# A planned attention kernel: another overlap for ScalarE in the planner, paddings moved in the opening, a new settings string

## The chip, the cores and the metric

The kernel runs on one core of a Trainium2 chip. The metric is the device time of one execution in microseconds; less is better. The time of the kernel before is the median of three runs.

## What is computed

The input is x, 2048 tokens of 512 numbers, in bfloat16. Two blocks are applied in turn, and the pair of them twice:

```python
x = x + A(layernorm(x), wqkv, wo)
x = x + B(layernorm(x), w1, b1, w2, b2)
x = x + A(layernorm(x), wqkv, wo)
x = x + B(layernorm(x), w1, b1, w2, b2)
```

A is softmax attention over all tokens with 32 heads of 16 numbers each: queries, keys and values come from one product with wqkv, the scores are scaled by 16 to the power -0.5, the probabilities weigh the values, and wo maps the result back. B is a product with w1 (512 by 1376), bias, tanh-approximated gelu, a product with w2, bias. The weights are the same in both rounds.

## The kernel before, in words

**Tiles.** Four heads make a head group; there are eight. Queries come in units of 512 tokens (smaller at the very end), keys in blocks of 128. One score tile is 128 keys by 512 queries of one head of a group. TensorE makes it with a 32-row product (line 1586) into a PSUM bank. There are 4096 such tiles in all.

**Two ways to the exponential.** Most tiles go to ScalarE: `flow_scores` takes them in groups, alternately of three banks and of two, and one ACTIVATE (line 1571) turns a group into probabilities in `PT`. Tiles whose key block is in `DK` (five of sixteen) can go to VectorE instead: `take_d` (line 1600) picks one, line 1678 writes its bits, and lines 1664, 1665, 1710, 1711 and 1719 add three shifted copies, which are used with scaled values `vs`. TensorE then multiplies probabilities with values (line 1805) and sums in bank `ACCB`. VectorE also does statistics, scaling and copies; GpSimd makes some shifts and the powers behind the layer norms.

**The order of the work.** Everything is planned when the kernel is built. `Sched` simulates five engine queues with durations written into the code, picks the earliest ready task with the lowest priority number, and writes the instructions of each engine in that order; on the chip every engine works its list in this order and waits on semaphores. A `Task` is submitted with its priority; `n0` (that is `now0`) puts an instruction into the list at once. `Prog.op` (line 109) computes when an engine is free again: the start plus the duration less `OVERLAP` of the engine (line 161). An exponential of n banks has the duration 0.19 + 0.4275 n. `best`, `stay` and `scores_due` use the same number to judge when ScalarE will want its next scores.

**The settings string.** `Hint.ORDER` has one digit for every four exponential groups (`STEP`, line 1504). A digit names an entry of `MODES`, which changes a few limits: how idle VectorE must be to be given a tile, when values are multiplied, how long other work may hold scores up. Digit 9 lets a group of three give one of its banks to a VectorE tile. A step beyond the string uses entry 0.

**Fills.** `refill` puts products of zeros (`zw`) into gaps of TensorE, into `ACCB` or a spare bank. Its `put` counts them at double duration while the plan's time is below `COLD`.

**The opening.** `build_startup` (line 808) issues the loads on SP in the order x tiles 0, 1, 2-3, weights of the keys, of the queries, of the values, x 4 to 9. GpSimd writes constants. The buffers `qk` 0 to 5 hold a tile's queries and keys, 16 numbers per head in 32 places, so the holes of 16 must be zero and one column of ones must stand in each key's hole: that is `pads` (line 845). GpSimd pads buffers 0 and 1, and ScalarE 2 to 5 with a copy of zeros (VectorE sets the ones); between them GpSimd sets the column of ones in V (line 862). Then come the statistics of x (line 983, 984), their scale on GpSimd (lines 991, 992), the scaling on VectorE (line 1003), transposes on TensorE (line 1161), their copy by ScalarE (line 1162), the products for keys, queries and values (line 1181), the keys' transposes by SP's DMA queue (line 1185), the bounds and scales of `job_scl`, the first scores and the first exponential. `job_first_tile` does this for tiles 0 to 3; each takes a `qk` buffer from the pool of line 736.

Of the kernel before, what the change touches and what calls it, by code (L numbers as in the profile page):

```python
# [13 lines left out]
ACTF = mybir.ActivationFunctionType  # L14
# [4 lines left out]
NDMAQ = 24  # L19
LATENCY = {"act": 0.033, "dve": 0.034, "pool": 0.083, "pe": 0.053, "sp": 0.06}  # L20
LAT_PE = 0.174
OVERLAP = {"act": 0.1415, "dve": 0.083, "pool": 0.014}
PE_SWITCH = 0.107
PE_ISSUE = 0.0035
DMA_MARGIN = 0.8
# [40 lines left out]
class Prog:  # L66
# [42 lines left out]
    def op(self, eng, fn, reads=(), writes=(), same_ok=(), dur=0.3, lat=None):  # L109
# [33 lines left out]
        else:  # L143
# [16 lines left out]
            op.t1 = op.t0 + dur  # L160
            self.free[eng] = op.t0 + (max(0.02, dur - OVERLAP[eng]) if lat is None else lat)
        deps = {}
# [121 lines left out]
def I(fn, reads=(), writes=(), dur=0.3, same_ok=(), lat=None):  # L284
    return (fn, tuple(reads), tuple(writes), tuple(same_ok), dur, lat)
# [9 lines left out]
class Sched:  # L295
# [147 lines left out]
    def stay(self, f, lim):  # L443

        P = self.P
        act = P.free["act"] + sum(max(0.02, o[4] - OVERLAP["act"]) for t in self.pend["act"] for o in t.ops)
        dve = P.free["dve"] + sum(o[4] for t in self.pend["dve"] if self.task_ready(t) <= f + D_NEAR for o in t.ops)
# [14 lines left out]
    def scores_due(self, f, lim):  # L462
# [7 lines left out]
        if first is None or first - f > HOLD_REACH:  # L470
            return None
        act = self.P.free["act"] + sum(max(0.02, o[4] - OVERLAP["act"]) for t in self.pend["act"] for o in t.ops)
        return max(first, act - HOLD_LEAD) + HINT.HOLD_LATE
# [67 lines left out]
FILL_LEAST = 96  # L541
FILL_MOST = 448
FILL_W = 3.414
COLD = 6.0
FILL_DT = 0.05
FILL_U = 0.55
FILL_SLACK = 0.02
# [12 lines left out]
ACCB = 6  # L560
# [28 lines left out]
class Hint:  # L589
    BASE = dict(D_IDLE=1.2, PV_LEAST=0.75, HOLD_LATE=0.4, PV_NEAR=0.7, LIN2=9, D_STEAL=0, POST=0, POOL_SHIFT=1, PV_DEEP=2, DEFER=0.0)  # L590
    MODES = (dict(), dict(D_IDLE=0.8), dict(D_IDLE=1.7), dict(PV_LEAST=0.6), dict(PV_LEAST=0.9), dict(HOLD_LATE=0.2), dict(HOLD_LATE=0.6), dict(PV_NEAR=0.4), dict(LIN2=0.9), dict(D_STEAL=1.0), dict(POST=1), dict(POST=2), dict(POOL_SHIFT=0), dict(DEFER=-2.0), dict(DEFER=0.2), dict(PV_DEEP=4, PV_LEAST=0.85), dict(PV_DEEP=3, PV_LEAST=0.8), dict(PV_DEEP=4, PV_LEAST=0.85, HOLD_LATE=0.7))
    STEP = 4
    ORDER = '5774500h8h000900700000440501000f04010f407c9f1c0hc700000b43cb00c4009084070hc200204040ccgg43c08f0900000c8c0cc0020c900342h003050234300373ffeda000h0004d2f00g30c3700700f0hgd0c9f5907e04h0770000h0203000000c003327h730000cf09277010g3047204c03f000de84c3025090fh9800c00000e9ec90f309020004803000c0000c9400c40g0cfh030009gf0003'

    def mode(self, k):
        self.__dict__.update(self.BASE)
# [2 lines left out]
    def at(self, step):  # L599
        self.mode(int(self.ORDER[step], 36) if step < len(self.ORDER) else 0)  # L600

# [5 lines left out]
class Builder:  # L607
# [45 lines left out]
    def alloc(self, es):  # L653
# [75 lines left out]
        pl = self.S_.pools  # L729
# [3 lines left out]
        pl["dp"] = Pool((0, 2, 4, 6) + tuple(range(12, NDP, 2)))  # L733
        pl["qraw"] = Pool(range(2))
        pl["qt"] = Pool(range(3))
        pl["qk"] = Pool(range(6))
        pl["vst"] = Pool([])
        pl["xn"] = Pool(range(3))
        pl["xnT"] = Pool(range(3))
# [68 lines left out]
    def build_startup(self):  # L808
        S, NT, NFC = self.S, self.NT, self.NFC
        n0 = self.now0  # L810
# [22 lines left out]
                self.S_.mark(("xld", a))  # L833
        self.S_.spawn(late(), 1.7)

        pool = lambda fn, writes, dur=0.4, reads=(): n0("pool", I(fn, reads, writes, dur))
        dve = lambda fn, reads, writes, dur=0.14: Task("dve", 1.9, [I(fn, reads, writes, dur)])
        pool(lambda e: e.memset(self.cneg[:, :], -0.5), [("cneg",)])
        pool(lambda e: e.memset(self.cstep.bitcast(U16)[:, :], SHIFT[1]), [("cstep",)])
# [5 lines left out]
        def pads(eng, b):  # L845
            qv = self.qks(b)
            hole = qv.rearrange("p k (h c) -> p (k h) c", c=32)[:, :, 16:32]
            ones = I(lambda e: e.memset(qv[:, 1, :].rearrange("p (h c) -> p h c", c=32)[:, :, 16:17], 1.0), [], [("qk", b, 0), ("qk", b, 1)], 0.1)
            if eng == "act":
                n0("act", I(lambda e: e.activation(out=hole, in_=self.zw[:, 0:16].unsqueeze(1).broadcast_to([128, 64, 16]), func=ACTF.Copy), [("zw",)], [("qk", b, 0), ("qk", b, 1)], 1.05))  # L850
                self.S_.submit(Task("dve", 1.3, [ones]))
            else:
                n0("pool", I(lambda e: e.memset(hole, 0.0), [], [("qk", b, 0), ("qk", b, 1)], 0.6),
                   I(ones[0], ones[1], ones[2], 0.2))
        n0("dve", I(lambda e: e.memset(self.zw[:, :], 0.0), [], [("zw",)], 0.2))
        n0("dve", I(lambda e: e.tensor_scalar(out=self.ident[:, :], in0=self.ioi, scalar1=0.0, scalar2=None, op0=ALU.is_equal), [("ioi",)], [("ident",)], 0.3))
        n0("dve", I(lambda e: e.memset(self.ps[:, ACCB, :], 0.0), [], [("ps", ACCB)], 0.57))  # L857
        self.P.free["act"] = 2.0
        vv = self.V[:, :, :, :, :].rearrange("p g k h d -> p (g k h) d")
        for b in (0, 1):  # L860
            pads("pool", b)
        n0("pool", I(lambda e: e.memset(vv[:, :, 16:17], 1.0), [], [("V", hg, kb) for hg in range(8) for kb in range(16)], 0.6))
        for b in range(2, 6):
            pads("act", b)

        def consts():
# [502 lines left out]
    def refill(self):  # L1369
# [5 lines left out]
        def add(act, t0, t1, w):  # L1375
            k = int(t0 / FILL_DT)
            while t0 < t1 - 1e-9:
                e = min(t1, (k + 1) * FILL_DT)
                act[k] += (e - t0) * w
                t0, k = e, k + 1  # L1380
# [23 lines left out]
        def put(b, how, p, w, st):  # L1404
            z = self.zero(b, how, p, w, st)
            x = P.op("pe", z[0], z[1], z[2], z[3], z[4] * (2.0 if P.free["pe"] < COLD else 1.0), z[5])
            add(real, x.t0, x.t1, 1.0 if how == "full" else 0.25)

        def fill(op):
# [8 lines left out]
            for t0, b, st, due in banks(op, start, t - op.t0)[:1]:  # L1418
                e = min(end, due)
                while True:  # L1420
                    rate = 1200.0 if t0 < COLD else 2400.0
                    w = min(FILL_MOST, int((e - t0) * rate))
# [814 lines left out]
```

## Time and profile before

| | |
|---|---|
| runs | 1533.81 us median of 3 (1532.12 to 1535.83) |
| profiled execution | 1530.92 us, of which the span of its instructions is 1529.1 us |
| TensorE busy | 1478.3 us (97%), fills among it |
| VectorE busy | 1388.9 us (91%) |
| ScalarE busy | 1493.3 us (98%) |
| GpSimd busy | 626.0 us (41%) |
| exponential groups on ScalarE | 1250, 1415.3 us |
| tiles on VectorE | 998 |

Busy time counts an instruction from start to end with overlaps counted once. In the groups, the number behind the bar is the busy time and the mean of one instruction in nanoseconds; behind the second bar stands the idle time just ahead of these instructions and what ended it. PE is TensorE, PEld its weight loads, DVE VectorE, ACT ScalarE, POOL GpSimd, SP the queue that issues the DMAs. PEclk is the clock granted to TensorE as a share of the full one.

### The profile page before, as it was taken

The page shows a single profiled execution, that of the slowest core. Times are in us where ns is not written, and L with a number is a line of the kernel's source. Part 1 is how long each engine was busy: PE and PEld are TensorE (multiplying, and loading weights), DVE is VectorE, ACT ScalarE, POOL GpSimd, SP SyncE. Part 2 cuts the span into 40 slices and gives each one's busy share as a digit, 9 for nine tenths or more (in the row PEclk, how much of TensorE's full clock was granted, in tenths as well). Part 3 has the DMA queues.
Part 4 walks back from the last instruction along what each step waited for, and adds up shares of the span by engine and source line. Part 5 has one row for each costly group of instructions (what it writes and reads, how often), then busy time and mean ns, then how long its engine had stood idle before and what let it go on. Part 6 is the DMA issues. An engine that isn't in the chain of part 4 may idle for free.

```text
span 1529.1 us, 49040 instructions
## 1 busy us (share of the span) xinstructions
PE 1478.3 (97%) x21518; PEld 516.5 (34%) x21518; DVE 1388.9 (91%) x2516; ACT 1493.3 (98%) x1339; POOL 626.0 (41%) x854
## 2 busy tenths in 40 slices
PE   8999999999999999999999999999999999999998
PEld 3322333333223322332233332223222332444664
DVE  7889999989999899989999798999999978998895
ACT  7999999999999999999999999999999999999996
POOL 4675653234343143434454437543444312441220
PEclk9999999999999999999999999999999999999999
DMA  5762111223221222213742332210011001120331
GB/s 154 123 143 76 57 32 36 57 32 87 78 50 46 48 79 60 57 36 90 135 81 63 61 89 56 63 35 13 22 36 36 20 24 31 40 44 19 81 64 27
DMA packets 212517, 91.05 MB, mean 60 GB/s; under 512 B 182251, under 2 KB 207184, under 8 KB 212304
## 3 DMA queue, kind: packets, MB, share of 16 engines
q1 hardware_dynamic: 212304, 87.92, 25.2%
q8 instruction: 168, 2.75, 0.8%
q14 instruction: 45, 0.37, 0.1%
HBM read 36.81 MB, written 19.48 MB: 37 GB/s over the span
## 4 chain that ended last, share of the span: by engine, by line
ACT 46%; PE 38%; DVE 13%; issue 2%; POOL 1%; DVEq 0%; POOLq 0%
ACT PT L1571 44%; PE ps L1586 12%; PE ps L1805 12%; PE ps L1892 11%; DVE dp L1678 5%; DVE dp L1719 2%; ACT h L2004 1%; PE ps L1479 1%; DVE dp L1665 1%; DVE st L983 1%; DVE accT L1835 1%; PE ps L1475 1%; DVE h L1981 0%; DVE dp L1710 0%; PE ps L1797 0%
## 5 line engine op out<-in xcount | busy, mean ns | idle before, releaser
L1571 ACT ACTIVATE PT<-ps 128x1536 bf16<-128x1536 f32 (+1 forms) x1250 | 1415.3, 1290 | 16.9 <-PE ps L1586 15.2
L1678 DVE TENSOR_SCALAR dp<-ps 128x512 uint16<-128x512 f32 x998 | 661.3, 681 | 76.6 <-PE ps L1586 68.7
L1586 PE MATMUL ps<-QT,KT 32*128 32x512 bf16 (+2 forms) x5120 | 597.4, 339 | 22.2 <-ACT PT L1571 8.6
L1711 POOL TENSOR_TENSOR dp<-dp,cstep 128x512 int32<-128x512 int32 x278 | 289.0, 1039 | 642.6 <-DVE dp L1678 417.2
L1805 PE MATMUL ps<-PT,V 128*17 128x512 bf16 (+2 forms) x3873 | 499.1, 339 | 2.7 <-issue 2.3
L1805 PE MATMUL ps<-dp,vs 128*17 128x512 bf16 (+2 forms) x3741 | 477.9, 338 | 1.2 <-issue 0.6
L1586 PEld LDWEIGHTS ps<-QT,KT 32*128 32x128 bf16 x5120 | 170.1, 91 | 516.4 <-ACT PT L1571 267.2
L1719 DVE TENSOR_SCALAR dp<-dp 128x2048 uint16<-128x2048 uint16 (+1 forms) x387 | 265.2, 694 | 5.8 <-POOL dp L1711 2.1
L1805 PE MATMUL ps<-dp,V 128*17 128x512 bf16 (+2 forms) x1247 | 233.2, 338 | 1.5 <-DVE accT L1835 0.9
L1805 PEld LDWEIGHTS ps<-dp,vs 128*17 128x17 bf16 x3741 | 133.2, 89 | 126.2 <-issue 90.4
L1805 PEld LDWEIGHTS ps<-PT,V 128*17 128x17 bf16 x3873 | 134.1, 89 | 97.8 <-issue 75.7
L1479 PE MATMUL ps<-zw 128*32 128x448 bf16 (+21 forms) x1627 | 166.8, 323 | 0.0
L1477 PE MATMUL ps<-zw 32*128 32x448 bf16 (+6 forms) x410 | 126.8, 333 | 0.0
L1892 PE MATMUL ps<-yT,wf 128*32 128x512 bf16 (+2 forms) x1720 | 109.3, 339 | 4.6 <-issue 2.4
L1892 PE MATMUL ps<-wqkv,xnT 128*32 128x512 bf16 x1392 | 101.4, 381 | 2.8 <-DVE dp L1678 0.8
L1311 POOL TENSOR_SCALAR QT<-qraw,scl,qbias 128x512 bf16<-128x512 bf16 (+2 forms) x91 | 76.7, 843 | 54.1 <-PE ps L1586 52.5
L1475 PE MATMUL ps<-zw 128*128 128x448 bf16 (+15 forms) x313 | 77.6, 333 | 4.7 <-DVE ps L857 3.0
L1665 DVE TENSOR_SCALAR dp<-dp 128x4096 uint16<-128x4096 uint16 x60 | 74.2, 1237 | 0.1
L1805 PEld LDWEIGHTS ps<-dp,V 128*17 128x17 bf16 x1247 | 60.3, 89 | 37.2 <-issue 18.5
L1479 PEld LDWEIGHTS ps<-zw 128*32 128x32 bf16 x1627 | 58.5, 95 | 21.4 <-issue 2.7
L1981 DVE TENSOR_SCALAR h<-ps,b1c 128x512 bf16<-128x512 f32 (+4 forms) x88 | 57.5, 654 | 8.5 <-PE ps L1892 7.8
L1835 DVE STREAM_TRANSPOSE accT<-ps 128x512 f32<-128x512 f32 (+2 forms) x96 | 59.4, 619 | 5.8 <-PE ps L1805 5.3
(202 smaller groups left out, 1119.6 us busy)
## 6 DMA issues: line engine op xcount, KB each, us to landing
vs<-vs_scr SPq DMA_DIRECT2D x64, 255.0 KB, 2.8
wf<-in_B_w_dram SPq DMA_DIRECT2D x90, 128.0 KB, 2.6
q_scr<-qk SPq DMA_DIRECT2D x20, 256.0 KB, 2.1
k_scr<-qk SPq DMA_DIRECT2D x12, 256.0 KB, 2.0
out_dram<-xres SPq DMA_DIRECT2D x16, 128.0 KB, 1.7
vs_scr<-vs SPq DMA_DIRECT2D x8, 255.0 KB, 3.1
xres<-in_A_x_dram SPq DMA_DIRECT2D x7, 256.0 KB, 5.5
v_scr<-vst SPq DMA_DIRECT2D x12, 136.0 KB, 2.3
```

Of the source, the lines that this page charges most:

```text
L1311: yield Task(eng, 0.4, [I(lambda e: e.tensor_scalar(out=self.QT[:, q, 0:W], in0=src, scalar1=self.scl[:, k, hg:hg + 1], scalar2=self.qbias ...
L1475: fn = lambda e: e.matmul(self.ps[:, b, 0:w], lhsT=self.zw[:, 0:128], rhs=self.zw[:, 0:w], start=st, stop=st, skip_group_check=True)
L1477: fn = lambda e: e.matmul(self.ps[:, b, 0:w], lhsT=self.zw[32 * p:32 * p + 32, 0:128], rhs=self.zw[32 * p:32 * p + 32, 0:w], start=st, sto ...
L1479: fn = lambda e: e.matmul(self.ps[32 * p:32 * p + 32, b, 0:w], lhsT=self.zw[:, 0:32], rhs=self.zw[:, 0:w], start=st, stop=st, skip_group_c ...
L1571: S_.submit(Task("act", 1e-5 * gi, [I(lambda e, pt=pt, n=n, b0=b0: e.activation(out=self.PT[:, pt:pt + n, :], in_=self.ps[:, b0:b0 + n, :] ...
L1586: return [I(lambda e, kb=kb, i=i: e.matmul(self.ps[:, b, i * W:(i + 1) * W], lhsT=self.KT[32 * hp:32 * hp + 32, hg, kb * 128:(kb + 1) * 12 ...
L1665: return lambda e: e.tensor_scalar(out=self.both(x[1], y[1]), in0=self.both(x[0], y[0]), scalar1=float(SHIFT[2]), scalar2=None, op0=ALU.add)
L1678: self.S_.submit(Task("dve", 0.0, [I(lambda e: e.tensor_scalar(out=self.dpu(u)[:, w * 512:(w + 1) * 512], in0=self.ps[:, b, :], scalar1=BI ...
L1711: lambda e: e.tensor_tensor(out=self.dpu(u + 1).bitcast(I32), in0=self.dpu(u).bitcast(I32), in1=self.cstep[:, 0:1].broadcast_to([128, 512] ...
L1719: t = Task("dve", prio(), [I(lambda e: e.tensor_scalar(out=self.dpp(v)[:, :, 0:N], in0=self.dpp(u)[:, :, 0:N], scalar1=float(SHIFT[2]), sc ...
L1805: ops.append((nth[j, sh] + 0.1 * i, I(lambda e, hp=hp, v=v, ap=ap[:, i * W:(i + 1) * W], first=first and i == 0, W=W: e.matmul(self.ps[32 ...
L1892: return [I(lambda e, j=j: e.matmul(self.ps[32 * j:32 * j + 32, b, 0:W], lhsT=lhsT(slice(32 * j, 32 * j + 32)), rhs=rhs(), start=start, st ...
```

## The change

The planner's overlap for ScalarE goes from 0.1415 to 0.128 us and `COLD` from 6.0 to 6.4. The settings string is another one, 312 digits instead of 313. In the opening, VectorE clears bank `ACCB` ahead of making the identity; V's ones are written by ScalarE, as a copy of a one-element constant, and not by GpSimd; buffers 0, 1, 4, 5 are padded by VectorE, buffer 0 at once and the others as tasks with priority 2.2 and more; ScalarE pads 2 and 3. The pool of `qk` buffers begins with 0, 2, 3, and 1, 4, 5 join it once they are padded. The planned duration of GpSimd's constants is 0.1 instead of 0.4.

```diff
-OVERLAP = {"act": 0.1415, "dve": 0.083, "pool": 0.014}
+OVERLAP = {"act": 0.128, "dve": 0.083, "pool": 0.014}
...
-COLD = 6.0
+COLD = 6.4
...
-    ORDER = '5774500h8h000900700000440501000f04010f407c9f1c0hc7...
+    ORDER = '57054000dh0003f3ff04f03207330700c002077c23c00ff4h0...
...
-        pl["qk"] = Pool(range(6))
+        pl["qk"] = Pool((0, 2, 3))
...
-        pool = lambda fn, writes, dur=0.4, reads=(): n0("pool", I(fn, reads, writes, dur))
+        pool = lambda fn, writes, dur=0.1, reads=(): n0("pool", I(fn, reads, writes, dur))
...
             else:
-                n0("pool", I(lambda e: e.memset(hole, 0.0), [], [("qk", b, 0), ("qk", b, 1)], 0.6),
-                   I(ones[0], ones[1], ones[2], 0.2))
+                zero = I(lambda e: e.memset(hole, 0.0), [], [("qk", b, 0), ("qk", b, 1)], 0.5)
+                if b == 0:
+                    n0("dve", zero, ones)
+                else:
+                    self.S_.submit(Task("dve", 2.2 + 0.01 * b, [zero, ones]), cb=lambda: self.S_.release("qk", b))
         n0("dve", I(lambda e: e.memset(self.zw[:, :], 0.0), [], [("zw",)], 0.2))
+        n0("dve", I(lambda e: e.memset(self.ps[:, ACCB, :], 0.0), [], [("ps", ACCB)], 0.48))
         n0("dve", I(lambda e: e.tensor_scalar(out=self.ident[:, :], in0=self.ioi, scalar1=0.0, scalar2=None, op0=ALU.is_equal), [("ioi",)], [("ident",)], 0.3))
-        n0("dve", I(lambda e: e.memset(self.ps[:, ACCB, :], 0.0), [], [("ps", ACCB)], 0.57))
         self.P.free["act"] = 2.0
         vv = self.V[:, :, :, :, :].rearrange("p g k h d -> p (g k h) d")
-        for b in (0, 1):
-            pads("pool", b)
-        n0("pool", I(lambda e: e.memset(vv[:, :, 16:17], 1.0), [], [("V", hg, kb) for hg in range(8) for kb in range(16)], 0.6))
-        for b in range(2, 6):
+        n0("dve", I(lambda e: e.memset(self.onec[:, :], 1.0), [], [("onec",)], 0.1))
+        n0("act", I(lambda e: e.activation(out=vv[:, :, 16:17], in_=self.onec[:, :].unsqueeze(1).broadcast_to([128, 512, 1]), func=ACTF.Copy), [("onec",)], [("V", hg, kb) for hg in range(8) for kb in range(16)], 2.38))
+        for b in (0, 1, 4, 5):
+            pads("dve", b)
+        for b in (2, 3):
             pads("act", b)
```

## Rows read from the trace of the kernel before

**Rows 1.** Profile page: the chain that ended last, shares of the span by line.

```profile
ACT PT L1571 44%; PE ps L1586 12%; PE ps L1805 12%; PE ps L1892 11%; DVE dp L1678 5%; DVE dp L1719 2%; ACT h L2004 1%; PE ps L1479 1%; DVE dp L1665 1%; DVE st L983 1%; DVE accT L1835 1%; PE ps L1475 1%; DVE h L1981 0%; DVE dp L1710 0%; PE ps L1797 0%
```

**Rows 2.** By stretches: each engine's busy us (instructions), then PEclk, DMA share, GB/s.

```profile
0.00:22.90 22.90, 16.71 (x95) 8.40 (x95) 17.38 (x53) 14.59 (x26) 8.29 (x22) 1.00 0.65 183
...
100.00:1450.00 1350.00, 1318.69 (x18040) 439.46 (x18036) 1250.28 (x2206) 1338.77 (x1184) 552.30 (x721) 1.00 0.23 54
...
6.60:8.40 1.80, 0.00 (x0) 0.00 (x0) 1.80 (x8) 0.00 (x0) 1.04 (x3) 1.00 1.09 365
```

**Rows 3.** Profile page, costliest groups: ScalarE's exponentials, VectorE's loads and shifts.

```profile
L1571 ACT ACTIVATE PT<-ps 128x1536 bf16<-128x1536 f32 (+1 forms) x1250 | 1415.3, 1290 | 16.9 <-PE ps L1586 15.2
L1678 DVE TENSOR_SCALAR dp<-ps 128x512 uint16<-128x512 f32 x998 | 661.3, 681 | 76.6 <-PE ps L1586 68.7
...
L1719 DVE TENSOR_SCALAR dp<-dp 128x2048 uint16<-128x2048 uint16 (+1 forms) x387 | 265.2, 694 | 5.8 <-POOL dp L1711 2.1
```

**Rows 4.** Timeline of ScalarE, 450 to 520 us: start, us, line, operation, count.

```profile
450.49 42.80 ACT L1571 ACTIVATE PT<-ps 128x1536 bf16<-128x1536 f32 x38 [0.28 <-PE ps L1586]
```

**Rows 5.** Groups by shape on ScalarE in that run of exponentials.

```profile
L1571 ACT ACTIVATE PT<-ps 128x1536 bf16<-128x1536 f32 x18 | 27.1, 1506 | 0.3 <-PE ps L1586 0.3
L1571 ACT ACTIVATE PT<-ps 128x1024 bf16<-128x1024 f32 x20 | 21.4, 1090 | 0.0
```

**Rows 6.** Waits: who for whom, total us, times, longest.

```profile
PEld ps L1586 <- DVE dp L1678: 63.4, 182, 0.9
...
ACT PT L1571 <- PE ps L1586: 15.2, 33, 1.9
```

**Rows 7.** Timeline of the opening: start, us, engine, line, operation, count, idle before.

```profile
0.84 0.24 DVE L855 MEMSET zw<- 128x224 uint32 x1 [0.84 <-PEq L2222]
...
1.21 1.17 DVE L856 TENSOR_SCALAR ident<-dp 128x128 bf16<-128x128 f32 x1
...
2.01 2.00 ACT L850 ACTIVATE h<-zw 128x1024 bf16<-128x1024 bf16 x2
2.11 1.57 SPq L818 DMA_DIRECT2D wqkv<-in_A_wqkv_dram  x3
...
3.03 3.54 PE L1475 MATMUL ps<-zw 128*128 128x448 bf16 x9 [3.03 <-DVE ps L857]
3.14 0.66 DVE L983 BATCH_NORM_STATS2 st<-xres 128x6 f32<-128x512 bf16 x1 [0.17 <-issue]
...
3.56 2.37 POOL L862 MEMSET V<- 128x512 bf16 x1
...
4.30 0.32 DVE L984 BATCH_NORM_AGGREGATE mv<-st 128x2 f32<-128x6 f32 x2
...
4.66 0.48 DVE L867 MEMSET dp<- 128x512 uint32 x1
...
6.02 0.19 POOL L991 TENSOR_SCALAR rs<-mv 128x1 f32<-128x1 f32 x1
...
6.29 0.60 POOL L992 TENSOR_TENSOR rs<-rs,cneg 128x1 f32<-128x1 f32 x1
...
8.00 0.38 DVE L1003 TENSOR_SCALAR dp<-xres,mv,rs 128x512 bf16<-128x512 bf16 x1
...
9.09 1.09 ACT L1162 ACTIVATE yT<-ps 128x512 bf16<-128x512 bf16 x2 [3.19 <-PE ps L1161]
...
9.83 1.87 PE L1181 MATMUL ps<-wqkv,yT 128*128 128x512 bf16 x4 [0.35 <-ACT yT L1162]
...
21.28 1.04 PE L1181 MATMUL ps<-wqkv,yT 128*128 128x512 bf16 x4
...
22.85 8.26 ACT L1571 ACTIVATE PT<-ps 128x1536 bf16<-128x1536 f32 x7
```

**Rows 8.** DMA issues of the opening: count, KB each, median us to landing.

```profile
wqkv<-in_A_wqkv_dram SPq DMA_DIRECT2D x3, 512.0 KB, 6.3
...
xres<-in_A_x_dram SPq DMA_DIRECT2D x2, 128.0 KB, 2.1
```

More of the change, by code (lines that the diff above doesn't have):

```diff
@@ L592 @@
     STEP = 4
-    ORDER = '5774500h8h000900700000440501000f04010f407c9f1c0hc700000b43cb00c4009084070hc200204040ccgg43c08f0900000c8c0cc0020c900342h003050234300373ffeda000h0004d2f00g30c3700700f0hgd0c9f5907e04h0770000h0203000000c003327h730000cf09277010g3047204c03f000de84c3025090fh9800c00000e9ec90f309020004803000c0000c9400c40g0cfh030009gf0003'
+    ORDER = '57054000dh0003f3ff04f03207330700c002077c23c00ff4h01004bb9cb9c1cc009803000e9g17h09700f0f04gb0804c00330c4fc8cg340cd00057h332ff0fc00aef000cca4053037d00f30200c007c01c4170gc0df72c40023c44g0030f0092d00000cdc0c700c00983c9h010c02019433c021cc9303g090g307h009f44b72ch00gb40c04d00c13ch3450513cdcc1900491c0b48090000d49470000'
     def mode(self, k):
```

## The prediction

> **What bounds the kernel now.** I read four views, from coarse to fine. The chain of waits [rows 1] runs through ScalarE's exponentials (line 1571) for 44% of the span; the matmul lines hold much of the rest because a group's scores stand just ahead of its exponential. The view by stretches [rows 2] says it more sharply: from 100 to 1450 us ScalarE works 1338.77 of 1350 us, so only 11.2 us are left idle there, while VectorE works 1250.28 and has 99.7 us free. In the first 22.9 us nothing is exponentiated at all; ScalarE works 14.59 of them. So the time is an opening of 22.9 us, then ScalarE's list of instructions back to back, then a tail that the diff doesn't touch. A gain can come from an earlier first exponential, from a shorter list (tiles handed to VectorE), or from ScalarE's 15.2 us of waiting for scores [rows 6].
>
> **Part 1, the opening.** In the timeline of the opening [rows 7] the reader should follow one chain: x's statistics are done (4.30 + 0.32 = 4.6), but GpSimd takes up the scale of tile 0 only at 6.02, because it is still writing V's ones (3.56 + 2.37 = 5.93). The scaling on VectorE starts at 8.00, ScalarE's copy of the transposed tile at 9.09, the first key product at 9.83, the first exponential at 22.85.
>
> Removed from GpSimd: two paddings with their ones, and V's ones. With them gone only short constants stand ahead of the scale, which then waits for the statistics alone. Two things replace it.
>
> VectorE takes paddings 0, 1, 4, 5. Padding 0 stands ahead of the statistics: start 0.84, zeros 0.24, the accumulator's zeros 0.5, the identity, one constant 0.1, the padding 0.5 (for it and the accumulator the 128x512 memset of 0.48 is the nearest row), its ones 0.1. The identity took 1.17 in a stretch where GpSimd wrote a padding; I take 0.38, which is what the scaling at 8.00 cost, with 1.17 as the other end. That ends at 2.7, or at 3.5. The statistics of x's tile 0 started at 3.14 with VectorE idle for 0.17 ahead of them, so x came just then: at 0.38 this wait covers the padding; at 1.17 the statistics slip by 0.4. Paddings 1, 4, 5 come with priority 2.2, behind statistics and constants: 3 x 0.6 = 1.8 us in a stretch where VectorE has 22.9 - 17.4 = 5.5 us free [rows 2]. If that cover fails, they cost up to 1.8; behind them stands the fourth tile, whose buffer 1 isn't free before.
>
> ScalarE loses paddings 4 and 5 (two take 2.00) and gains V's ones. No row shows that write on ScalarE: the ends are 0.6 (a 128x512 tile on it, as at 9.09: two in 1.09) and 2.37 (GpSimd, the same scattered write). I take the upper, since it is the same pattern. Then ScalarE is free at 2.0 + 2.4 + 2.0 = 6.4, otherwise at 4.6.
>
> New chain: scale at 4.6 instead of 6.02, its two GpSimd instructions 0.9 as before (6.02 to 6.9), scaling at 5.5, plus 1.09 to ScalarE's copy = 6.6 (ScalarE is free at 6.4), plus 0.74 to the key product = 7.3. What is late next: the key weights. Their issue starts at 2.11; the three weights have one landing figure, 6.3 [rows 8]. As the third one's (three issues in 1.57, so its own starts near 3.2) it means 9.5, and two loads of 0.52 MB at 365 GB/s [rows 2] take 2.9, so the first lands at 6.6. Ends: 4.2 (the 2.1 of x's tiles) and 9.5. At 6.6 it doesn't bind. So the key product comes at 7.3 instead of 9.83: 2.5 us. Bounds: 0.4 if the weights bind at 9.5, 3.2 if all is in time at 6.6.
>
> **The clock.** The first four key products take 1.87, four alike at 21.28 take 1.04, all in stretches where the granted-clock column reads 1.00. The spacing tells more than the column: nine fills of 448 columns take 3.54, that is 0.39 each, the 1.2 GHz level; TensorE then stands from 6.57 to 8.45. The accumulator's zeros now come ahead of the identity, so fills can start at 1.6 instead of 3.03 and last until the transposes. If that brings the key products to 2.4 GHz, it adds 1.87 - 1.04 = 0.8. The fills here didn't bring it over the pause, so I leave it out of the sum and keep it as the upper end, and as a rival. The Trainium skill (TensorE: Matmul & The Clock Gate, What's actually happening) says that the default is the slow clock and that activity releases it; by that rule the opening gives 3.3 instead of 2.5.
>
> From the first key product to the first exponential are 13.0 us, which I leave as they are: statistics of keys, queries, the DMA transposes on SP and the scale all shift along; the number of SP's instructions is unchanged. Opening: -2.5, between -4.0 (3.2 + 0.8) and +1.4 (0.4 gained, 1.8 lost to the paddings).
>
> **Part 2, the account and the string.** OVERLAP is what the planner takes off an exponential's duration for the start of the next. 18 three-bank and 20 two-bank groups [rows 5] ran in 42.80 [rows 4]. By the code a group is 0.19 + 0.4275 per bank, together 47.41; with 37 overlaps the old constant gives 42.17, the new 42.67. The new one fits. Over 1250 groups the planner had ScalarE 1250 x 0.0135 = 16.9 us too early. With the same instructions the constant changes nothing on the chip; it works through the order that the planner writes.
>
> What the order can win: an exponential costs 1415.3 / 1250 = 1.13 us a group [rows 3], with 2.5 tiles in a group on average 0.45 per tile. A tile on VectorE costs it (661.3 + 265.2) / 998 = 0.93 us, from the same groups. If the planner sees ScalarE 16.9 us longer, balance returns at 16.9 / (0.45 + 0.93) = 12 tiles moved, worth 5.5 us, against 99.7 us free. Second reading: the string has one digit for four groups; 313 digits for 1250 groups before, 312 after, so at most 1248 and at least 1245 groups: 2 to 5 fewer, 2.3 to 5.7 us, provided tiles per group stay (the digit that shrinks groups, 9, stands 15 times before, 16 times after). I take the middle of this, -4.0; the ends are 0 (the length says nothing) and -5.7, and -7.6 more if half of the 15.2 us of waiting goes.
>
> From the same rows the overlap is (47.41 - 42.80) / 37 = 0.125. The Trainium skill (ScalarE: Activation LUTs, What ACT_TABLE_LOAD costs) says that back-to-back activations overlap by about 93 ns; by that the new constant would leave the planner 0.035 x 1250 = 44 us short, still misjudging ScalarE. The trace disagrees with it, at 125.
>
> COLD, the GpSimd duration and the smaller qk pool are the planner's alone; they cost nothing beside what is counted.
>
> **Sum.** -2.5 - 4.0 = -6.5 on the profiled execution's 1530.92 gives 1524.4. The median of the runs shown is 2.9 above that execution, so I put the forecast at 1533.8 - 6.5 = 1527.3. About 0.2% (3.1 us) is what a measurement of this kernel can tell from no change.
>
> **Rivals.** (a) *Opening alone*: the new order wins and loses alike, and only -2.5 stays: 1531.3, no change to be told. For it: ScalarE has 11.2 us idle in 1350, little to win without moving tiles. Against: the digits. Chance 0.15. (b) *An account still short*: waits hide in the 42.80 us the other way, the real spacing is wider than the new constant, the order stays as ill-fitting as it was, and again 1531.3. Against it: 42.67 and 42.80 are 0.3% apart. Chance 0.05. The Trainium skill's 93 ns, cited above, would be this case. (c) *Late weights*: the key weights land at 9.5, the opening gives 0.4, the order 4.0: 1529.4. Chance 0.10. (d) *Fast clock from the start*: the longer fills bring the key products to 2.4 GHz, 0.8 more: 1526.5. For it: fills could start 1.4 us earlier; against it: they ran 3.54 us before and the products were still slow. Chance 0.12. The Trainium skill's clock gate, cited above, speaks for it. (e) *More tiles moved*: 20 tiles rather than 9 go into VectorE's free 99.7 us: -2.5 - 20 x 0.45 = -11.5, 1522.3. Chance 0.10. (f) *Slower*: more VectorE tiles put more of their scores ahead of ScalarE's groups in TensorE's fixed order. TensorE already waits 182 times on VectorE's loads, and ScalarE 33 times for scores, 15.2 / 33 = 0.46 us each [rows 6]. If these double, +15.2 - 6.5 = +8.7: 1542.5. It decides from 14 more such waits (14 x 0.46 = 6.4), and is told from no change from 21. Against it: an account that fits makes late arrivals rarer. Chance 0.13. The forecast keeps 0.35.
>
> Faster: 0.35 + 0.10 + 0.12 + 0.10 = 0.67; same 0.15 + 0.05 = 0.20; slower 0.13. The range goes from 1533.8 - 4.0 - 5.7 - 7.6 = 1516.5, put at 1517, to 1533.8 + 1.4, put at 1535; it leaves out (f) and little else.
>
> **What would show it.** Right: GpSimd's first scale near 4.6, ScalarE free near 6.4, first key product near 7.3, first exponential near 20.3; 1245 to 1248 groups and some 1003 to 1010 VectorE tiles; ScalarE's waits for scores at or below 15.2. V's ones far above 2.4 would show the opening step wrong; a first exponential at 22 with the key product at 7.3 would show that the chain behind it sets the opening. More than 1250 groups, or waits for scores above 22, would make the prediction wrong.

## The result and the profile after

The kernel after takes 1536.61 us (median of 20 executions, 1533.98 to 1539.54); the kernel before took 1533.98 us beside it (20 executions, 1531.98 to 1536.79). The ratio is 1.0016, interval 1.0009 to 1.0023: slower by about 2.5 us, inside the 0.2% that I called indistinguishable, and outside the range given, on the side where the prediction had left rival (f) out. The profiled execution of after took 1538.27 us (span 1536.2), 1.7 above its median, while that of before lies 3.1 below its own. So the two traces differ by more than the two kernels do, and what follows rests on pairs of rows and on medians, not on the two spans.

Four lines of the page of after answer to [rows 1, 3]: the chain by line, then the groups (busy us, mean ns | idle before them, and who ended it).

```profile
ACT PT L1575 21%; PE ps L1590 15%; PE ps L1809 14%; PE ps L1896 13%; DVE dp L1682 11%; DVE dp L1723 3%; DVE dp L1669 2%; PE ps L1479 2%; PE ps L1483 1%; ACT h L2008 1%; DVE st L987 1%; DVE accT L1839 1%; DVE dp L1714 1%; PE ps L1185 1%; DMA yT<-xn 1%
...
L1575 ACT ACTIVATE PT<-ps 128x1536 bf16<-128x1536 f32 (+1 forms) x1247 | 1414.9, 1266 | 26.6 <-PE ps L1590 22.8
L1682 DVE TENSOR_SCALAR dp<-ps 128x512 uint16<-128x512 f32 x1009 | 669.3, 681 | 73.4 <-PE ps L1590 65.2
...
L1723 DVE TENSOR_SCALAR dp<-dp 128x2048 uint16<-128x2048 uint16 (+1 forms) x368 | 255.6, 699 | 4.4 <-POOL dp L1715 2.2
```

The code stands four lines lower than before. VectorE is busy 1403.2 us (1388.9 before), ScalarE 1493.1 (1493.3), GpSimd 599.2 (626.0). The counts are those forecast: 1247 groups, 1009 VectorE tiles. But the chain of work that ended last spends 21% of the span in the exponentials where it spent 44%, and 11% in VectorE's loads where it spent 5%; the idle time ahead of the exponentials is 26.6 us instead of 16.9. Their busy time has hardly fallen (1415.3 to 1414.9): three groups fewer, but 593 of three banks and 654 of two where there were 599 and 650.

The waits of after (who for whom, us, times, longest), beside [rows 6]:

```profile
PEld ps L1590 <- DVE dp L1682: 71.9, 192, 1.6
...
ACT PT L1575 <- PE ps L1590: 22.8, 41, 1.7
...
PE ps L1590 <- DVE dp L1682: 8.7, 22, 1.1
```

The last line has this counterpart before:

```profile
PE ps L1586 <- DVE dp L1678: 2.5, 10, 0.4
```

So a score product itself waited for VectorE to empty its bank 22 times instead of 10, and 8.7 us instead of 2.5. ScalarE has eight more waits for scores, and 7.6 us more in them. This view shows only part of it. ScalarE's instructions overlap, so a group that comes late by less than the overlap makes no idle time. The spacing of ends shows it: in every trace here the ends stand 1.344 us apart (median) for three banks and 0.917 for two. What a spacing has beyond this I call a stall (I count 0.05 to 3 us; sixteen of each trace's count hold a short instruction of ScalarE's own, under 3 us together, and the seven longer breaks come to 57.6 us in after and in e2 alike). Before has 128 stalls of 30.4 us together, after 176 of 44.1. The list itself became shorter: six three-bank groups, four two-bank groups and a single one exchanged give 6 x 1.344 - 4 x 0.917 + 0.49 = 4.9 us less.

The opening of after (timeline; start, us, engine, line, operation, count, idle before), beside [rows 7]:

```profile
0.84 0.24 DVE L858 MEMSET zw<- 128x224 uint32 x1 [0.84 <-PEq L2226]
...
1.19 0.48 DVE L859 MEMSET ps<- 128x512 f32 x1
...
1.58 0.21 DVE L860 TENSOR_SCALAR ident<-dp 128x128 bf16<-128x128 f32 x1
...
1.73 3.60 PE L1479 MATMUL ps<-zw 128*128 128x448 bf16 x11 [1.73 <-DVE ps L859]
...
1.85 0.48 DVE L853 MEMSET qk<- 128x512 uint32 x1
2.02 2.38 ACT L864 ACTIVATE V<-onec 128x512 bf16<-128x512 bf16 x1
...
2.64 0.48 DVE L871 MEMSET dp<- 128x512 uint32 x1
...
3.19 0.48 DVE L853 MEMSET qk<- 128x512 uint32 x1
...
3.75 0.66 DVE L987 BATCH_NORM_STATS2 st<-xres 128x6 f32<-128x512 bf16 x1
...
3.92 2.26 ACT L850 ACTIVATE h<-zw 128x1024 bf16<-128x1024 bf16 x2
...
5.18 0.19 POOL L995 TENSOR_SCALAR rs<-mv 128x1 f32<-128x1 f32 x1 [3.78 <-DVE mv L988]
...
6.05 0.67 DVE L987 BATCH_NORM_STATS2 st<-xres 128x6 f32<-128x512 bf16 x1
...
6.65 0.39 DVE L1007 TENSOR_SCALAR dp<-xres,mv,rs 128x512 bf16<-128x512 bf16 x1
...
7.10 0.89 PE L1165 MATMUL ps<-ident,dp 128*128 128x128 bf16 x8 [1.77 <-DVE dp L1007]
...
7.53 1.09 ACT L1166 ACTIVATE yT<-ps 128x512 bf16<-128x512 bf16 x2 [1.34 <-PE ps L1165]
...
8.27 3.43 PE L1185 MATMUL ps<-wqkv,yT 128*128 128x512 bf16 x9 [0.29 <-ACT yT L1166]
...
21.51 2.35 ACT L1575 ACTIVATE PT<-ps 128x1536 bf16<-128x1536 f32 x2
```

The first key product comes at 8.27 instead of 9.83, the first exponential at 21.51 instead of 22.85. The nine products that come first (eight of 512 columns for keys, one of 128 for queries) take 3.43 us, and most start 0.43 apart. By stretches (busy us and instructions of PE, PEld, DVE, ACT, POOL; then the granted clock, DMA share, GB/s) the clock is seen at half here, and once more at 98 us:

```profile
8.00:10.00 2.00, 1.73 (x5) 0.66 (x6) 1.49 (x10) 0.62 (x2) 0.90 (x2) 0.50 1.09 373
...
98.00:100.00 2.00, 2.00 (x13) 0.32 (x12) 1.93 (x5) 1.28 (x1) 0.94 (x1) 0.50 0.59 125
100.00:1450.00 1350.00, 1311.71 (x18107) 436.74 (x18108) 1259.69 (x2211) 1333.71 (x1177) 528.73 (x697) 1.00 0.24 54
```

In 100 to 1450 us ScalarE is busy 1333.71 us instead of 1338.77 [rows 2]: it idles 16.3 us where it idled 11.2.

### The profile page after: what moved, and what is told of

The parts are those of the page before. It is cut to its first block, busy times and chain, and to the rows that moved or that the text cites. A ratio compares the mean times of both kernels' runs of the same rounds, so it can differ in the third digit from the quotient of the medians.

```text
span 1536.2 us, 49457 instructions
## 1 busy us (share of the span) xinstructions
PE 1478.1 (96%) x21736; PEld 517.4 (34%) x21736; DVE 1403.2 (91%) x2547; ACT 1493.1 (97%) x1335; POOL 599.2 (39%) x829
## 4 chain that ended last, share of the span: by engine, by line
PE 47%; DVE 24%; ACT 23%; issue 3%; POOL 2%; DMA 1%; POOLq 0%; SPq 0%; DVEq 0%
ACT PT L1575 21%; PE ps L1590 15%; PE ps L1809 14%; PE ps L1896 13%; DVE dp L1682 11%; DVE dp L1723 3%; DVE dp L1669 2%; PE ps L1479 2%; PE ps L1483 1%; ACT h L2008 1%; DVE st L987 1%; DVE accT L1839 1%; DVE dp L1714 1%; PE ps L1185 1%; DMA yT<-xn 1%
## 5 line engine op out<-in xcount | busy, mean ns | idle before, releaser
L1575 ACT ACTIVATE PT<-ps 128x1536 bf16<-128x1536 f32 (+1 forms) x1247 | 1414.9, 1266 | 26.6 <-PE ps L1590 22.8
L1715 POOL TENSOR_TENSOR dp<-dp,cstep 128x512 int32<-128x512 int32 x258 | 267.7, 1038 | 683.5 <-DVE dp L1682 417.2
L1809 PE MATMUL ps<-PT,V 128*17 128x512 bf16 (+2 forms) x3865 | 509.2, 339 | 1.2 <-issue 1.0
L1809 PE MATMUL ps<-dp,vs 128*17 128x512 bf16 (+2 forms) x3765 | 491.1, 339 | 3.0 <-issue 1.8
L1723 DVE TENSOR_SCALAR dp<-dp 128x2048 uint16<-128x2048 uint16 (+1 forms) x368 | 255.6, 699 | 4.4 <-POOL dp L1715 2.2
L1483 PE MATMUL ps<-zw 128*32 128x448 bf16 (+18 forms) x1887 | 186.4, 320 | 0.3 <-DVE dp L1682 0.3
L1481 PE MATMUL ps<-zw 32*128 32x448 bf16 (+5 forms) x373 | 118.6, 336 | 0.0
L1669 DVE TENSOR_SCALAR dp<-dp 128x4096 uint16<-128x4096 uint16 x71 | 88.5, 1246 | 0.1
L1479 PE MATMUL ps<-zw 128*128 128x448 bf16 (+19 forms) x284 | 69.7, 333 | 4.7 <-DVE dp L1682 1.7
L1483 PEld LDWEIGHTS ps<-zw 128*32 128x32 bf16 x1887 | 65.6, 95 | 21.7 <-DVE dp L1682 3.7
L1714 DVE TENSOR_SCALAR dp<-dp 128x1024 uint16<-128x1024 uint16 (+1 forms) x170 | 71.7, 427 | 0.9
L1340 POOL TENSOR_SCALAR vs<-V 128x340 bf16<-128x340 bf16 (+2 forms) x72 | 64.5, 896 | 8.0 <-DMA V<-v_scr 2.2
```

Source lines behind the costliest of these rows:

```text
L1479: fn = lambda e: e.matmul(self.ps[:, b, 0:w], lhsT=self.zw[:, 0:128], rhs=self.zw[:, 0:w], start=st, stop=st, skip_group_check=True)
L1481: fn = lambda e: e.matmul(self.ps[:, b, 0:w], lhsT=self.zw[32 * p:32 * p + 32, 0:128], rhs=self.zw[32 * p:32 * p + 32, 0:w], start=st, sto ...
L1483: fn = lambda e: e.matmul(self.ps[32 * p:32 * p + 32, b, 0:w], lhsT=self.zw[:, 0:32], rhs=self.zw[:, 0:w], start=st, stop=st, skip_group_c ...
L1575: S_.submit(Task("act", 1e-5 * gi, [I(lambda e, pt=pt, n=n, b0=b0: e.activation(out=self.PT[:, pt:pt + n, :], in_=self.ps[:, b0:b0 + n, :] ...
L1669: return lambda e: e.tensor_scalar(out=self.both(x[1], y[1]), in0=self.both(x[0], y[0]), scalar1=float(SHIFT[2]), scalar2=None, op0=ALU.add)
L1714: t = Task(eng, prio() if eng == "dve" else 0.6, [I((lambda e: e.tensor_scalar(out=self.dpu(u + 1)[:, 0:N], in0=self.dpu(u)[:, 0:N], scala ...
```

## The experiments

Experiments are named e1 to e11. They ran in three groups (e1 to e4, e5 to e8, e9 to e11), each with the kernel before beside it; ratios are to that one, and where two groups are compared, both medians and ratios are given. "Old string" and "new string" are the two values of the settings string, each with its own planner constant unless said otherwise.

**e1, the kernel before once more.** No edit.

> The kernel before, once more, for a second trace and for the granted clock of several of its runs (those of after had 0.996 to 1.000, mean 0.998). If the loss of after came with dips of TensorE's clock that its order brings (rival), the runs here show 1.000 throughout; if dips are common to both (theory: they are not the cause), some runs here show 0.997 to 0.999 as well. Time: 1534.0, ratio 1.000 within 0.001.

Measured: 1534.86 us, ratio 1.0001 (0.9990 to 1.0012). First exponential 22.78, 125 stalls of 30.8 us, ScalarE's waits 16.4 us, 31 times: up to 1440 us the stalls repeat from execution to execution, almost window by window. The mean granted clock of its executions is 0.998 to 1.000, of before's own beside it 0.997 to 1.000, of after's 0.996 to 1.000: dips are common to both kernels, as the theory had it.

**e2, the new opening alone.** The changed kernel with the constant and the string of before:

```diff
-OVERLAP = {"act": 0.128, "dve": 0.083, "pool": 0.014}
+OVERLAP = {"act": 0.1415, "dve": 0.083, "pool": 0.014}
-    ORDER = '57054000dh00...'
+    ORDER = '5774500h8h00...'
```

> The kernel before with the new opening, with the old overlap (0.1415) and the old string. Theory (the opening gains, the new order loses more): the first exponential at 21.5 as in after, 1250 groups, 998 VectorE tiles, and the time lower by the 1.3 us of the earlier first exponential: 1532.7, ratio 0.9991. Rival (the new opening is what costs, through the paddings and the clock that falls at 7.9 us): ratio 1.001 or more.

Measured: 1531.94 us, ratio 0.9982 (0.9974 to 0.9991): faster by 2 to 3 us. The timeline of its opening:

```profile
8.28 1.94 PE L1185 MATMUL ps<-wqkv,yT 128*128 128x512 bf16 x9 [0.29 <-ACT yT L1166]
...
20.61 3.70 ACT L1575 ACTIVATE PT<-ps 128x1536 bf16<-128x1536 f32 x3
```

The first key product stands where after has it, but the nine take 1.94 us instead of 3.43, and the first exponential comes at 20.61, not at the 21.5 that I had expected. TensorE's list up to there is the same in both kernels; it ran at the other clock level.

**e3, the new account and string alone.** The kernel before with the two lines of the changed kernel (the reverse of e2's edit, on the old opening).

> The kernel before with the new overlap (0.128) and the new string, and the old opening. Theory: first exponential at 22.9, 1247 groups, 1009 VectorE tiles, ScalarE's waits for scores above 20 us, time 1534.0 + 2.6 + 1.3 = 1537.9, ratio 1.0026. Rival (the opening costs, the order is neutral): 1534 or less, ratio at most 1.000.

Measured: 1539.05 us, ratio 1.0032 (1.0019 to 1.0046): slower by 5 us. 179 stalls, 46.2 us; ScalarE waits 24.2 us, 43 times. e2 and e3 add up: -0.0018 + 0.0032 = +0.0014, measured +0.0016. So the opening gains nearly what it should, and the new order loses almost twice that. The profiled execution of e3 (1542.73) is the slowest of its seven. Its first exponential comes at 24.00, where I had expected 22.9: its products of 512 columns stand 0.43 us apart until 14.9 us, those of before 0.22 from 12.7 on, so most of this delay is the clock level's.

**e4, the new constant with the old string.**

```diff
-OVERLAP = {"act": 0.1415, "dve": 0.083, "pool": 0.014}
+OVERLAP = {"act": 0.128, "dve": 0.083, "pool": 0.014}
```

> The kernel before with the new overlap alone, the old string kept. If overlap and string can be judged apart (my prediction's way, the overlap worth some 5 us), between 1528 and 1540. If the string fits only the plan that it was found for, so that any other constant throws it off, the time is far higher: the same steps with other moments to choose at, over 1560, with fewer VectorE tiles than 998 and more groups than 1250.

Measured: 1594.71 us in its one execution, 61 above before. Its group of exponentials on the page:

```profile
L1571 ACT ACTIVATE PT<-ps 128x1536 bf16<-128x1536 f32 (+1 forms) x1257 | 1436.0, 1261 | 58.9 <-PE ps L1586 54.5
```

There are more groups, fewer VectorE tiles (976) and 54.5 us of waiting. The old string does not fit the plan that the other constant gives. Here constant and string are one part, and the question is whether the new pair is better than the old one.

**e5 and e6, VectorE relieved, new and old order (both with the new opening).** The double shift writes half of its columns, in an order that stays the same, so the output lacks the other half (GpSimd writes zeros once for what is never written, which delays the first exponential to 23.8 and 24.1 us, in both nearly alike):

```diff
-out=self.dpp(v)[:, :, 0:N], in0=self.dpp(u)[:, :, 0:N], scalar1=float(SHIFT[2])
+out=self.dpp(v)[:, :, 0:N // 2], in0=self.dpp(u)[:, :, 0:N // 2], scalar1=float(SHIFT[2])
```

> The kernel after, but the double shift on VectorE (line 1723) works on half of its columns, with the plan and every list unchanged; the buffers are zeroed once by GpSimd in the opening. The output lacks half of those shifted probabilities. It takes about 0.27 us from each of some 370 instructions, 98 us of VectorE's 1403. Theory (the new order's loss is lateness of VectorE, which its order has no room for): ScalarE's waits for scores fall well below 22.8, the time to 1519 to 1526, and below that of the same edit in the old order. Rival (the loss sits in TensorE's own order or its clock): the time stays within 4 us of 1536.6, and stays 4 to 5 above the same edit in the old order.

> The same halved shift in the kernel of e2 (old overlap, old string, new opening). Theory: it gains less than the new order does, 4 to 8 us from 1531.9, that is 1524 to 1528, so that the new order becomes the better one by 1 to 5 us. Rival: both gain alike and the old order stays ahead by 4 to 5.

Measured: e5 1524.31 us, ratio 0.9942 (0.9925 to 0.9960); e6 1528.16 us, 0.9957 (0.9941 to 0.9973), just above its range. VectorE's busy time falls by 76.5 us in e5 (1403.2 to 1326.7) and 78.4 in e6 (1389.3 to 1310.9), less than the 98 that I had expected. With VectorE relieved the new order is no longer 5 us worse but 2 to 4 better. The two intervals overlap, so the sign alone is not certain; the swing of 7 us and more is clear of the noise. The stretch 100 to 1450 us and ScalarE's waits of e5:

```profile
100.00:1450.00 1350.00, 1316.49 (x18536) 440.15 (x18529) 1200.30 (x2242) 1342.72 (x1189) 516.20 (x708) 1.00 0.24 55
```

```profile
ACT PT L1579 <- PE ps L1594: 11.9, 26, 1.7
...
DVE rv L1869 <- POOL accT L1867: 2.8, 3, 1.2
```

VectorE works 1200.30 us there instead of 1259.69, and ScalarE's waits fall from 22.8 us to 11.9 (e6: 13.5, 25 times). Stalls: 26.7 us (e5) and 25.0 (e6). The shorter list of 4.9 us was there all along; it shows once VectorE isn't late. The last line is VectorE's waiting for GpSimd's combine (see e10): it is the same 2.8 us, 3 times, as in after, so the relief did not work by shortening these waits.

**e7 and e8, VectorE burdened, new and old order (new opening).** A memset of one byte, called ahead of each double shift:

```diff
+    def extra(self, e):
+        self.nextra += 1
+        return e.memset(self.spill[:, self.nextra - 1:self.nextra], 0)
```

> The kernel after with one more short instruction on VectorE (a memset of one byte per partition, some 0.06 us) ahead of each double shift, unplanned, some 300 of them, 20 us of VectorE's work in all. Theory: with no room on VectorE it costs the new order more than the old: 8 to 14 us, 1545 to 1551. Rival (VectorE has 99 us free and lateness there isn't the cause): under 3 us, and alike in both orders.

> The same extra instructions in the kernel of e2. Theory: 4 to 9 us, 1536 to 1541, less than in the new order, so the distance between the orders grows beyond 4.7 us. Rival: under 3 us, the distance stays.

Measured: e7 1539.08 us (ratio 1.0034, 1.0025 to 1.0044), e8 1534.26 (1.0009, 0.9995 to 1.0024). That is 2.5 to 2.8 us more than after and 2.3 to 4.1 more than e2 (by medians and by ratios). My expectation of a larger loss under the new order fell; the rival's "alike" was met, so this pair does not support my theory over it. The dose was small: the 368 memsets of e7 last 21.7 us together, but VectorE's busy time rose by 4.6 us only (1403.2 to 1407.8; in e8 by 6.2), since a memset mostly overlaps its neighbour. Still, about half of this or more reached the end, although VectorE had some 90 us free between 100 and 1450 us.

**e9, fills up to the transposes.** The kernel of e2 with

```diff
-COLD = 6.4
+COLD = 3.0
```

> The kernel of e2 (new opening, old account, old string) with COLD 3.0: the same instructions in the same order but 17 instead of 11 fill matmuls of 448 columns in the opening, so that TensorE works on to the transposes instead of standing for 1.77 us. Clock theory: the profile of the changed kernel and that of e2 differ in the nine key products (3.43 us against 1.94) because TensorE's clock came or fell by chance around that pause; without the pause the nine take under 2.1 us in this profile too, the first exponential stands at 20.6 or before, and the time is 1530.0 to 1532.0. Rival (the opening's clock is worth nothing, the chain behind sets it): 1531 to 1533, no difference from e2. Against both: the fills run late and hold the transposes up, first key product after 8.6, time 1532.5 to 1534.

Measured: 1531.98 us, ratio 0.9987 (0.9978 to 0.9995), no different from e2. Timeline of TensorE:

```profile
7.45 0.61 PE L1165 MATMUL ps<-ident,dp 128*128 128x128 bf16 x8
8.62 1.94 PE L1185 MATMUL ps<-wqkv,yT 128*128 128x512 bf16 x9 [0.56 <-ACT yT L1166]
```

The fills hold the transposes up by 0.35 us, the nine products take 1.94 us, the first exponential comes at 20.73 (the clock theory asked for 20.6). Both theories' ranges hold the time, so it decides nothing about what the pause is worth.

**e10 and e11, GpSimd's combine shortened, new and old order (new opening).** The two large instructions that join the two halves of an output keep their places but work on 16 of 256 columns, so the output lacks the rest of one half; the second of them is shown:

```diff
-out=T[:, :, 0:16], in0=T[:, :, 0:16], in1=M, op=ALU.add
+out=T[:, 0:1, 0:16], in0=T[:, 0:1, 0:16], in1=M[:, 0:1], op=ALU.add
```

What led to it stands in the trace of after, around one of the two largest stalls between 120 and 360 us (1.14 us at 220, 1.09 at 189; the five larger ones lie elsewhere, and the largest, 1.8 us at 84, is in e2's trace too):

```profile
183.05 1.11 DVE L1723 TENSOR_SCALAR dp<-dp 128x2048 uint16<-128x2048 uint16 x1
183.58 0.67 POOL L1861 TENSOR_TENSOR den<-den,dw 128x16 f32<-128x16 f32 x1
...
184.63 0.73 POOL L1863 TENSOR_TENSOR accT<-accT,dp 128x256 f32<-128x256 f32 x1
...
185.40 0.25 DVE L1865 RECIPROCAL rv<-accT 128x16 f32<-128x16 f32 x1 [1.23 <-POOL accT L1863]
185.57 2.49 DVE L1682 TENSOR_SCALAR dp<-ps 128x512 uint16<-128x512 f32 x4
...
186.25 0.38 PE L1590 MATMUL ps<-QT,KT 32*128 32x512 bf16 x1 [1.11 <-DVE dp L1682]
...
187.33 2.37 ACT L1575 ACTIVATE PT<-ps 128x1536 bf16<-128x1536 f32 x2 [0.98 <-PE ps L1590]
```

Read it downwards: VectorE's next instruction is a reciprocal of the combined output, and it waits 1.23 us for GpSimd; behind it on VectorE stand four score loads; TensorE's next scores need the bank that the first of them empties and wait 1.11 us; ScalarE's scores stand behind these in TensorE's list, and ScalarE waits 0.98 us.

> The changed kernel with GpSimd's two large instructions of the two-part combine on the first 16 of 256 columns (the other columns of the first part are then left out of the output); order and planned times unchanged. In the traces VectorE waits 3 times, 2.8 us, for this combine under the new order and 2 times, 1.5 us, under the old. Theory (VectorE is late by its own full list, GpSimd is a small part of it): 1533.5 to 1536.5, ScalarE's waits for scores 18 to 23 us. Rival (the new order's loss comes through GpSimd's combine, which the traces show ahead of the two largest of ScalarE's stalls): 1531 to 1533, waits for scores near 15.

> The same shortening in the kernel of e2 (new opening, old account and string, 1531.9). Theory: 1529.5 to 1532, so a gain within 1.5 us of the one under the new order. Rival (the loss of the new order comes through the combine): 1531 to 1532, a gain of under 1 here against 3.6 to 5.6 there.

Measured: e10 1531.71 us, ratio 0.9989 (0.9980 to 0.9997), so 4 to 5 us under the changed kernel; e11 1529.70, 0.9973 (0.9964 to 0.9983), 1.4 to 2.2 us under e2. The same place in e10, timelines of ScalarE and of VectorE:

```profile
182.54 8.43 ACT L1575 ACTIVATE PT<-ps 128x1536 bf16<-128x1536 f32 x7
...
183.06 0.25 DVE L1865 RECIPROCAL rv<-accT 128x16 f32<-128x16 f32 x1 [0.72 <-POOL accT L1863]
```

VectorE waits 0.72 us instead of 1.23, and ScalarE goes through without a gap. ScalarE's waits of e10, then of e11:

```profile
ACT PT L1575 <- PE ps L1590: 16.8, 35, 1.7
```

```profile
ACT PT L1575 <- PE ps L1590: 16.9, 29, 1.9
```

For e10 the rival's range (1531 to 1533) holds the time and my own doesn't. VectorE's waits for the combine fell from 2.8 us to 0.7 in e10, and from 1.5 to nothing in e11, so under the new order the gain is larger than the waiting removed. The edit also took 16.8 us of work from GpSimd (599.2 to 582.4) and 2.5 from VectorE (1403.2 to 1400.7), and these runs don't separate the two ways. For e11 neither text fits well: the gain is larger than the rival's "under 1", and 2.7 us smaller than e10's where I had written within 1.5. The measurement of that difference is about as uncertain as its size. The stalls, which repeat closely in executions of one order, say it more firmly: 44.1 to 37.4 us under the new order, 34.7 to 31.3 under the old.

**The account of it all.** Worked out from the ends of the exponentials; the columns are the number of stalls, their sum (us), the part of it behind VectorE, the part between 120 and 360 us, and the start of the first exponential (us). "Behind VectorE" asks which engine ended most of TensorE's idle time in the 2.5 us ahead of the late group:

```
                              stalls   sum  VectorE  120-360  first
before                           128  30.4      8.8      3.0  22.85
e1  before again                 125  30.8      8.6      3.0  22.78
e2  old order, new opening       128  34.7      8.2      3.1  20.61
e8  the same, burdened           140  34.3      9.7      3.7  21.47
e11 as e2, short combine         127  31.3      7.7      1.9  20.59
e6  as e2, VectorE relieved      108  25.0      5.3      1.4  24.08
after, new order                 176  44.1     17.0      9.6  21.51
e3  new order, old opening       179  46.2     18.9      9.4  24.00
e7  new order, burdened          186  45.5     18.0     10.4  21.43
e10 new order, short combine     171  37.4     13.7      6.8  21.42
e5  new order, VectorE relieved  131  26.7      7.4      4.9  23.84
```

From e2 to after: 4.9 us shorter list, 9.4 us more stalls, 0.9 us later first exponential = +5.4, where the spans differ by 5.9 and the medians by 4.7. Of the 9.4 us, 6.6 lie between 120 and 360 us, and 8.8 are behind VectorE (6 to 11, as one looks back 1.5 to 4 us). The 0.9 us are the clock level of the opening and not the order: e8 has the old order, slow key products and its first exponential at 21.47. From before to e2 the traces show 4.3 us more stalls, 3.0 of them behind 1440 us, so what the opening gained is read from the first exponential and from the medians, not from these two spans.

## Why the prediction was wrong

**The opening gained nearly what was forecast, in part by luck.** Forecast -2.5; e2 gives -2.1 by medians, -2.8 by the ratio, and its trace 22.85 - 20.61 = 2.24. Step by step: V's ones on ScalarE cost 2.38 us (taken: 2.37) and ScalarE was free near 6.2 (6.4). The padding cost 0.48 and 0.09, the identity 0.21, below the 0.38 that I took for it. The key weights were there in time: the first key product waited for ScalarE's copy alone. Two steps came later than said. I read priority 2.2 as behind the statistics, but another buffer's zeros at 2.64 and padding 1 at 3.19 stood ahead of them in VectorE's list, and the scale began at 5.18 instead of 4.6. Then the third tile's statistics (6.05, 0.67 us) stood ahead of the scaling, which began 1.47 us behind the scale instead of 0.9. So the first key product came at 8.27, not 7.3. What I left out gave it back in e2's trace: at the higher clock level the first nine products took 1.94 us. That is rival (d), and it came by chance: the same list of TensorE ran them in 1.94 us in e2 and e11, in 3.18 in e8, which has e2's string and constant too, and in 3.43 and 3.07 in after and e10, with the first exponential 0.8 to 0.9 us later. The prediction named this term as 0.8 and left it out of its sum. So the size is right in part by luck: the chain that I worked out gave 1.56 us at the first key product instead of 2.5.

**The step that failed is "the order -4.0".** What it said of the plan is true: the new constant fits (1.344 and 0.917 us are 0.19 + 0.4275 n - 0.128 within two nanoseconds), 1247 groups, 1009 tiles, a list shorter by 4.9 us. What it said of the time is false: the same order costs 5 us on the chip (e3; after against e2). The sum put the change in ScalarE's waiting at nothing; the traces of e2 and after show 9.4 us more stalls against the 4.9 us of the shorter list, and 8.8 of them behind VectorE. The working booked 12 tiles of 0.93 us (11 came) "against 99.7 us free" of VectorE. That free time is a sum over 1350 us. It says nothing of the places where VectorE has a queue of loads and TensorE's fixed list stands behind the first of them. There a delay of VectorE passes through a score bank to ScalarE within 2 us, as the stall at 187 us shows. The relief of e5 and e6 shows the mechanism: take time from VectorE, and the new order's loss of 5 us is gone, with the stalls behind VectorE down from 17.0 us to 7.4. e10 and e11 point to one source of the delays, GpSimd's combine: between the orders it makes about half of the loss by the medians (2.7 us, uncertain by as much) and a third of the stalls (9.4 us become 6.1). The rest stays with VectorE's own queue, in places that I haven't told apart.

**Rival (f) had the mechanism, and the sign, and the wrong price.** It asked for 14 more waits; there were 8, so it would have counted this as a gain. The row that priced it shows only lateness beyond ScalarE's overlap. In spacings the late groups went from 128 to 176. The sign of being wrong that the prediction gave, waits for scores above 22, did come true, at 22.8.

**Rivals (a), (b), (c), (e).** (a) put the order at nothing; it costs 5. (b) falls: the new account is exact. The overlap of 0.125 us that the prediction read holds against the code's durations; against the recorded means of [rows 5] (1506 and 1090 ns) the same run gives 0.165. What the trace fixes is the spacing. (c) falls: no wait for weights. (e) had the count of tiles too high, and its sign falls with the same step as mine.

**A rival that I hadn't named**, dips of the clock: the profile of after has one at 96 to 100 us, and e1 has its own near the end. The four executions of after with a mean granted clock of 1.000 average 1535.4 us, the 21 of before (beside e1 to e11) 1533.5: without dips about 2 of the 2.6 us are left, so they aren't what puts it behind before.

The version to keep is e2: the new opening with the old constant and string, 1531.94 us, ahead of both kernels by 2 us and more.

## What to carry to other kernels

Free time of an engine, summed over a long stretch, is no room for more work: ask at each place what stands behind that engine's queue, and how fast its delay reaches the engine that sets the end. A truer constant in a planner doesn't give a better order by itself; a settings string and the constant that it was found with are best treated as one setting (e4 lost 61 us by parting them), and a hand edit that comes together with such a new pair must be timed without it. Where instructions overlap, count lateness by the spacing of their ends: the idle column misses what the overlap swallows.

## What the runs showed of the hardware

A scattered write of single elements, 128x512 in steps of 17, cost ScalarE 2.38 us, the same as GpSimd's 2.37 before.

VectorE and GpSimd hold each other up in places. The identity took 1.17 us before [rows 7], beside this memset, and 0.21 in after, where GpSimd writes nothing large there:

```profile
1.36 0.94 POOL L853 MEMSET qk<- 128x1024 bf16 x1
```

In e10 a GpSimd product of only 16 columns took 1.29 us (its mean there is 0.34), beginning at the same moment as a VectorE addition of 4096 columns:

```profile
180.50 1.22 DVE L1669 TENSOR_SCALAR dp<-dp 128x4096 uint16<-128x4096 uint16 x1
...
180.50 1.29 POOL L1860 TENSOR_TENSOR dp<-dp,dw 128x16 f32<-128x16 f32 x1 [1.61 <-ACT dw L1859]
```

The Trainium skill (SBUF — State Buffer, SBUF: two separate sides) describes a pair of ports that GpSimd shares with VectorE instructions of certain kinds as locked for a whole instruction by whichever starts first, while the other fully blocks. The two rows agree: GpSimd's small product ended 0.07 us behind VectorE's long addition.

The traces of e10 and e11 show it 27 times. Of their 128 instructions of 16 columns in the combine, 101 took 0.21 to 0.27 us, many of them beside a score load of VectorE; the other 27 took 0.34 to 1.29, and each ended 0.07 to 0.09 us behind a VectorE instruction that works from SBUF to SBUF, 23 times one of the shifts (lines 1668, 1669, 1723). So a combine on GpSimd is longest where VectorE has such work, and in the place shown from after VectorE then waits for it.

The same list of TensorE, with a pause of 1.1 to 1.8 us ahead of the transposes, ran the opening's first products at either clock level from one execution to the next. The granted clock reads 0.50 from 8 to 10 us for the 3.43 us of after and 1.00 for the 1.94 us of e2, but 1.00 too for the 3.07 us of e10 and the 3.18 of e8, where these products stand 0.43 us apart as in after: the spacing tells the level more surely than the record.
